# Scoring the diagonal and far ends of a sliding window together with whole key tiles, as tiles of 32 by 64

## The chip, the cores and the metric

The kernel runs on one core of a Trainium2 chip. The metric is the time of one execution on the device in microseconds; the median of a few runs counts. The core has a matrix engine (PE, with its weight loads listed apart as PEld), a vector engine (DVE), a scalar engine that makes the exponentials (ACT), a general engine (POOL) and a queue that issues most transfers (SP). They run at the same time and wait for each other by semaphores; each takes its own instructions in order. Matrix products write to PSUM, the other tensors lie in SBUF.

## The reference

Two attention layers over 2048 tokens, 640 wide, 32 heads of 20, whose outputs stand side by side.

```python
# A: four segments of 512 tokens; causal softmax inside a segment, and a memory of the segments before
logits = einsum('bhqd,bhkd->bhqk', qs, ks) * scale + mask
a_dot = einsum('bhqk,bhkd->bhqd', softmax(logits), vs)
a_mem = (phi(qs) @ M) / (phi(qs) @ z + 1e-6)
o = g * a_mem + (1.0 - g) * a_dot          # g = sigmoid(beta), one for each head
M = M + phi(ks)^T @ vs;  z = z + sum(phi(ks))
# B: sliding window of 256 keys
mask = (i - j >= 0) & (i - j < 256)
p = softmax(where(mask, q @ k^T * scale, -1e9));  o = p @ v
# both: out = o @ wo
```

## The kernel before

The work is cut into eight chunks of 512 tokens, in the order A0, B0, A1, B1, A2, B2, A3, B3. For each chunk the queries, keys and values are projected (`qk_job`, `v_job`), scores are made, turned into exponentials and masked (`score_batch`, `mask`), multiplied by the values (`av`, `av_tile`), transposed and divided by the sum (`turn`, `norm`), and projected to the output (`final`, `final_job`). Projections of the next chunk and output projections of earlier ones are put between the scores of the present chunk.

Heads have 20 rows, so four heads lie in the four row groups of 32 of the matrix engine; there are eight such groups of four heads. One **visit** of `score_batch` takes two PSUM tiles `sc` of 128 by 2 by 512 (three exist), runs score matmuls for the four heads of one or more groups into up to 512 columns of each head, and then one exponential on ACT for each of the two tiles. The results are two tiles `pt` (ten exist), in which masks set the forbidden scores to zero.

In B the keys are stored shifted by 64, so that a whole key tile `("f", u)` covers the keys from 64 before query block u to its middle. A query block of 128 needs two whole tiles of 128 keys and two **ends**: the upper half of its own diagonal, 64 keys by its last 64 queries (`"l"`, into PSUM rows 0 to 63), and the far 64 keys by its first 64 queries (`"u"`, into rows 64 to 127). Whole tiles run as matmuls on tiles of 32 rows by 128 columns of the engine, ends as tiles of 32 by 64.

For chunks B0 to B2, `batches` makes five visits for each pair of groups. In the order of issue they are

```python
(g0,   f0 256 queries, f3 128, f-1 128)   # f-1 not in chunk 0
(g0,   f1 256,         f2 256)
(both, ends of all four query blocks)      # 16 entries of 64 queries, 64 matmuls
(g0+1, f0, f3, f-1)
(g0+1, f1, f2)
```

After the third visit the first group's value product may run, after the fifth the second's. In whole-tile visits two kinds of mask are selects on POOL (line 862): `near`, at the lower edge of the diagonal, and `far`, at the far edge of the window, each over two blocks of 64 queries and both heads of a tile, 256 elements. The ends are masked by one multiply on DVE (line 840) with a table `ends`. A's chunks and B's last chunk have visits of ends alone too; there the change leaves the work as it is.

The order of all matrix work is written out in `PLAN`, a list that the main loop of `body` follows: `S` and `s` are the next visit, `A` the next value product, `M` the next memory product, `q30*5` five matmuls of that projection, and so on. An `A` behind an `S` makes the projections after it run as four column tiles of 128 by 32, the shape that the value product has, in place of one of 128 by 128; that saves a change of shape and issues four times the instructions. Each engine gets its instructions in the order in which this loop emits them; what isn't in the list (masks, copies, divisions, transfers) is placed by a running estimate, `Flow`, that holds assumed times of every engine.

Lines named below: 807 the score matmuls, 823 the exponentials, 862 the selects, 840 the multiplies of ends, 876 and 898 the value products, 929 and 924 the projections (as one matmul and as four column tiles), 943 the transposes, 981 the products with the reciprocal sum.

Of the kernel before, what the change touches and what calls it, by code (L numbers as in the profile page):

```python
# [13 lines left out]
P = 128  # L14
H = 32
DH = 20
# [251 lines left out]
class _K:  # L268
# [526 lines left out]
    def score_batch(self, n, ent, kof, q, masks):  # L795
# [3 lines left out]
        cols = 0  # L799
        for g, ref, q0, nq, c0 in ent:  # L800
            k, kc = kof(ref)
            h0, h1 = {"a": (0, P), "f": (0, P), "l": (0, SH), "u": (SH, P), "s": (0, SH),
                      "t": (SH, P)}[ref[0]]
            k0 = kc + (h0 if ref[0] != "t" else 0)
            for j in range(4):
                rows = slice(HD * j, HD * j + DH)
                nc.tensor.matmul(ps[j // 2][h0:h1, j % 2, c0:c0 + nq],  # L807
                                 lhsT=k[rows, g, k0:k0 + h1 - h0],
                                 rhs=q[rows, g, q0:q0 + nq],
                                 start=True, stop=True, tile_position=(HD * j, h0),  # L810
                                 skip_group_check=ref[0] in "lust")
# [22 lines left out]
    def mask(self, m, pt, te, ready, x):  # L834
        nc, f = self.nc, self.f
        kind, c0, n = m
        if kind == "ends":
            def go():
                blk = pt[:, :, 0:n].rearrange("p h (b c) -> p h b c", c=SH)
# [15 lines left out]
        else:  # L855
            blk = pt[:].rearrange("p h (b c) -> p h b c", c=2 * P)[:, :, 0:n, c0:c0 + SH]
# [320 lines left out]
    def batches(self, chunks):  # L1177
# [5 lines left out]
        near = lambda n: ("near", 0, n)  # L1183
        far = lambda n: ("far", P + SH, n)
        for n, (kind, c) in enumerate(chunks):
            if kind == "A":
                for g0, ng, at in SQUARES0 if c == 0 else SQUARES:
                    for g in range(g0, g0 + ng):
                        for ent in BANKS_A:
                            out.append([n, [(g, ("a", kt), P * kt + SH, L - P * kt - SH, c0)  # L1190
                                            for kt, c0 in ent], [("part", c0, SH) for _, c0 in ent], []])
                        if g == g0 + at:
# [3 lines left out]
                                        [("ends", 1, P * ng)], []])  # L1196
# [7 lines left out]
            if n == len(chunks) - 1:  # L1204
                for qt in range(LT):
                    for g0 in (0, 2, 4, 6):
# [5 lines left out]
                        if g0 == 2:  # L1212
                            out.append([n, [e for g in range(G) for e in ends(g, qt, SH * g)],
                                        [("ends", 0, L)], [(qt, 0)]])
# [494 lines left out]
```

## Time and profile before

| what | us |
|---|---|
| median of three runs | 329.65 |
| the runs | 329.33, 329.65, 332.19 |
| the profiled execution | 332.08 |
| its span, first to last instruction | 330.4 |
| PE busy | 319.3 |
| ACT busy | 300.2 |
| POOL busy | 266.4 |
| DVE busy | 256.9 |

The profile is one execution. Busy time of PE is the union of its matmuls, each with its latency, so it doesn't say that PE streams all that time; the other engines run one operation at a time. A row of the timeline has the start and the length of one or more like instructions, then the engine, the line, the operation and the shapes, with the idle time before it in brackets and what ended it. PE's granted clock was 0.995 of full speed over the span. The chunks show in the operands of the scores: B0 is scored from 47 to 90 us, B1 from 126 to 170, B2 from 204 to 246, B3 from 280 on.

### The profile page before, as it was taken

To read this page: it belongs to the slowest core of one execution; us is meant where nothing else is said; L and a number is where in the kernel's file an instruction comes from. 1 tells how busy PE (TensorE), PEld (TensorE's weight loads), DVE (VectorE), ACT (ScalarE), POOL (GpSimd) and SP (SyncE) were. 2 spreads that over 40 slices of the span, in tenths; PEclk is the share of its full clock that TensorE was granted. 3 is DMA by queue.
4 is the path that set the end of the run, shared out by engine and by line. 5 is a ranking of instruction groups with operands and counts; after the bars stand their busy time and mean duration, and the time that the engine had idled before them with its cause. 6 is when DMAs were issued, how large, how long until landed. Compare 5 with 4: busy or idle time off the path is not lost.

```text
span 330.4 us, 17022 instructions
## 1 busy us (share of the span) xinstructions
PE 319.3 (97%) x7218; PEld 177.5 (54%) x7218; DVE 256.9 (78%) x537; ACT 300.2 (91%) x334; POOL 266.4 (81%) x676
## 2 busy tenths in 40 slices
PE   8999999999999999999999999999999999979995
PEld 2455546455544455656654546456754545646673
DVE  6777667789887878898868887889667798846673
ACT  2889899899999997999999999899999999949972
POOL 8376679988759989987877999998976899958870
PEclk9999999999999999999999999999999999979999
DMA  6985854743568867264699146057674064577412
GB/s 188 406 257 136 190 148 107 170 138 65 116 164 180 183 146 209 45 138 114 170 170 221 35 87 183 8 113 161 146 175 100 11 178 125 117 190 167 101 64 81
DMA packets 73449, 47.12 MB, mean 143 GB/s; under 512 B 47229, under 2 KB 70045, under 8 KB 73373
## 3 DMA queue, kind: packets, MB, share of 16 engines
q1 hardware_dynamic: 72653, 45.38, 55.8%
q8 instruction: 56, 0.92, 1.2%
q10 hardware_dynamic: 720, 0.66, 0.7%
q14 instruction: 20, 0.16, 0.2%
HBM read 17.62 MB, written 16.79 MB: 104 GB/s over the span
## 4 chain that ended last, share of the span: by engine, by line
PE 61%; POOL 16%; ACT 8%; issue 7%; DVE 4%; DMA 3%; POOLq 0%; ACTq 0%; DVEq 0%
PE m L929 30%; PE sc L807 13%; POOL pt L862 10%; PE m L924 9%; PE m L876 8%; ACT pt L823 7%; POOL o L981 3%; DMA wv_A<-in_A_wv_dram 2%; POOL u L981 2%; DVE tt L943 1%; ACT e L577 1%; DMA wk_A<-in_A_wk_dram 1%; PE m L686 1%; DVE pt L840 1%; POOL pkS L668 1%
## 5 line engine op out<-in xcount | busy, mean ns | idle before, releaser
L823 ACT ACTIVATE pt<-sc 128x1024 bf16<-128x1024 f32 (+2 forms) x306 | 283.4, 1017 | 14.6 <-PE sc L807 12.4
L862 POOL TENSOR_SCALAR_AFFINE_SELECT pt<-pt 128x128 bf16<-128x128 bf16 (+1 forms) x512 | 178.8, 378 | 49.2 <-ACT pt L823 42.5
L943 DVE STREAM_TRANSPOSE tt<-m 128x512 f32<-128x512 f32 x88 | 61.5, 711 | 24.2 <-PE m L876 13.4
L981 POOL TENSOR_TENSOR o<-tt,rr 128x320 bf16<-128x320 f32 x64 | 48.4, 756 | 4.6 <-DVE rr L971 3.9
L807 PE MATMUL sc<-qB,kB 20*64 20x64 bf16 (+2 forms) x1728 | 40.8, 218 | 2.7 <-issue 2.0
L840 DVE TENSOR_TENSOR pt<-pt,ends 128x1024 bf16<-128x1024 bf16 (+2 forms) x50 | 37.4, 758 | 0.0
L1093 DVE CAST ot<-m 128x320 bf16<-128x320 f32 x58 | 27.8, 484 | 11.6 <-PE m L929 9.9
L807 PEld LDWEIGHTS <-kB 20*64 20x64 bf16 (+1 forms) x1728 | 22.6, 99 | 25.6 <-issue 23.2
L929 PEld LDWEIGHTS <-xT 128*128 128x128 bf16 x295 | 26.4, 97 | 18.2 <-issue 6.3
L807 PE MATMUL sc<-qA,kA 20*64 20x64 bf16 (+4 forms) x1024 | 34.2, 237 | 0.2 <-issue 0.2
L929 PEld LDWEIGHTS <-oT 128*128 128x128 bf16 x239 | 21.5, 99 | 11.3 <-issue 1.6
L807 PEld LDWEIGHTS <-kA 20*128 20x128 bf16 (+1 forms) x1024 | 14.0, 97 | 21.9 <-issue 19.9
L929 PE MATMUL m<-wBv,xT 128*128 128x320 bf16 x145 | 24.0, 299 | 1.1 <-DVE tt L943 0.6
L876 PE MATMUL m<-pt,vA 128*32 128x192 bf16 (+3 forms) x512 | 23.6, 274 | 0.0
L929 PE MATMUL m<-wo_A,oT 128*128 128x320 bf16 x131 | 23.2, 312 | 0.0
L929 PE MATMUL m<-wv_A,xT 128*128 128x320 bf16 x130 | 22.0, 300 | 0.3 <-DMA wv_A<-in_A_wv_dram 0.3
L929 PE MATMUL m<-xT,wq_A 128*128 128x512 bf16 x85 | 21.5, 380 | 0.7 <-DMA wq_A<-in_A_wq_dram 0.6
L929 PE MATMUL m<-xT,wBk 128*128 128x512 bf16 x84 | 21.5, 381 | 0.0
L929 PE MATMUL m<-xT,wBq 128*128 128x512 bf16 x77 | 20.3, 380 | 0.0
L738 DVE CAST vB<-m 128x320 bf16<-128x320 f32 x32 | 15.6, 487 | 4.7 <-PE m L929 2.4
L557 DVE CAST kB<-m 128x512 bf16<-128x512 f32 x20 | 13.7, 686 | 6.4 <-PE m L929 4.6
L981 POOL TENSOR_TENSOR u<-tt,rr 128x320 bf16<-128x320 f32 x24 | 18.0, 753 | 0.2
(127 smaller groups left out, 458.6 us busy)
## 6 DMA issues: line engine op xcount, KB each, us to landing
out_dram<-ot SPq DMA_DIRECT2D x29, 160.0 KB
scr_o<-o SPq DMA_DIRECT2D x28, 160.0 KB
xT<-in_B_x_dram SPq DMA_DIRECT2D x8, 288.0 KB
xT<-in_A_x_dram SPq DMA_DIRECT2D x8, 256.0 KB
scr_pk<-e SPq DMA_DIRECT2D x15, 128.0 KB
vS<-vA SPq DMA_DIRECT2D x16, 87.0 KB
vL<-vB SPq DMA_DIRECT2D x8, 174.0 KB
vU<-vB SPq DMA_DIRECT2D x14, 87.0 KB
```

The source lines that it names most:

```text
L557: nc.vector.tensor_copy(out=dst[:, m, at:at + L], in_=ps[:, :])
L738: nc.vector.tensor_copy(out=dst, in_=src)
L807: nc.tensor.matmul(ps[j // 2][h0:h1, j % 2, c0:c0 + nq], lhsT=k[rows, g, k0:k0 + h1 - h0], rhs=q[rows, g, q0:q0 + nq], start=True, stop=Tr ...
L823: nc.scalar.activation(out=pt[:, :, lo:hi], in_=ps[i][:, :, lo:hi], func=ACT.Exp, scale=self.scale)
L840: nc.vector.tensor_tensor(out=blk, in0=blk, in1=self.ends[:, c0, :].unsqueeze(1).unsqueeze(1) .to_broadcast([P, 2, n // SH, SH]), op=ALU.mult)
L862: nc.gpsimd.affine_select(out=blk, in_=blk, pattern=pat, compare_op=ALU.is_ge, fill=self.zero, base=base, channel_multiplier=mul)
L876: nc.tensor.matmul(O[HD * j:HD * j + HD, q0:q0 + nq], lhsT=v[:, at:at + HD], rhs=pts[j // 2][:, j % 2, c0:c0 + nq], start=(n_ == 0), stop= ...
L924: self.nc.tensor.matmul(ps[s, 0:n], lhsT=lhsT[:, s], rhs=rhs, start=start, stop=stop, tile_position=(0, HD * j), skip_group_check=True)
L929: self.nc.tensor.matmul(ps[:, 0:n], lhsT=lhsT, rhs=rhs, start=start, stop=stop, skip_group_check=True)
L943: self.nc.vector.transpose(out=tt[:], in_=O[:, :])
L981: nc.gpsimd.tensor_tensor(out=to[:] if add_to else to, in0=a, in1=b, op=ALU.mult)
L1093: nc.vector.tensor_copy(out=ot[:, 320 * hf:320 * hf + 320], in_=ps[:, 0:320])
```

## The change

For chunks B0 to B2 the five visits of a pair become

```python
(g0,   f1 256, f3 128,  ends of query blocks 0 and 1)
(g0,   f2 256, f-1 128, ends of query blocks 2 and 3)   # f-1 not in chunk 0
(both, f0 256 of each group)
(g0+1, f1, f3, ends of 0 and 1)
(g0+1, f2, f-1, ends of 2 and 3)
```

In a visit that has ends, whole key tiles are scored as two halves of 64 keys, so that the whole visit is in tiles of 32 by 64: 16 matmuls for two whole key tiles and 16 for four ends. The third visit has whole tiles alone, on tiles of 32 by 128. The mask of ends is multiplied into 128 of a tile's columns from a given start, and `near` and `far` get the step between their blocks as a parameter, with one or two blocks each. The assumed time of visits on tiles of 32 by 64 is another one, and `PLAN` is another list, with the same number of each kind of entry but for one `S` that became `s`.

```diff
 PLAN = (
-    "q00*5 k00*5 k01*5 s q01*5 v00*4 S v00*14 s v00*2 q02*3 S q02*2 q03*5 k02*3 S k02*2 k03*5 "
...
+    "k00*5 q00*5 q01*5 S k01*5 v00*5 S v00*10 s v00*5 k02*5 s q02*5 k03*3 S k03*2 q03*5 k04*5 A "
...
+        by_half = ent[-1][1][0] in "lust"
         for g, ref, q0, nq, c0 in ent:
             k, kc = kof(ref)
-            h0, h1 = {"a": (0, P), "f": (0, P), "l": (0, SH), "u": (SH, P), "s": (0, SH),
-                      "t": (SH, P)}[ref[0]]
-            k0 = kc + (h0 if ref[0] != "t" else 0)
-            for j in range(4):
-                rows = slice(HD * j, HD * j + DH)
-                nc.tensor.matmul(ps[j // 2][h0:h1, j % 2, c0:c0 + nq],
-                                 lhsT=k[rows, g, k0:k0 + h1 - h0],
...
+            halves = {"l": (0,), "s": (0,), "u": (SH,), "t": (SH,)}.get(ref[0], (0, SH) if by_half else (0,))
+            w = SH if by_half else P
+            for h0 in halves:
+                k0 = kc + (h0 if ref[0] != "t" else 0)
+                for j in range(4):
+                    rows = slice(HD * j, HD * j + DH)
+                    nc.tensor.matmul(ps[j // 2][h0:h0 + w, j % 2, c0:c0 + nq],
+                                     lhsT=k[rows, g, k0:k0 + w],
...
-        if ent[0][1][0] in "lust":
-            t = f.on_pe("row64", 40.0 * len(ent), cols / 2, 0.0, 4 * len(ent))
+        if by_half:
+            ends = sum(e[1][0] in "lust" for e in ent)
+            mms = 4 * (2 * len(ent) - ends)
+            ns = max(20.8 * ends + (cols - SH * ends) / 2.4 + 5.0, 0.0 if mms <= 32 else 8.35 * mms - 8.0)
+            t = f.on_pe("row64", ns, cols / 2, 0.0, mms)
...
-                blk = pt[:, :, 0:n].rearrange("p h (b c) -> p h b c", c=SH)
+                blk = pt[:, :, at:at + n].rearrange("p h (b c) -> p h b c", c=SH)
...
-            blk = pt[:].rearrange("p h (b c) -> p h b c", c=2 * P)[:, :, 0:n, c0:c0 + SH]
+            x0 = c0 // at
+            blk = pt[:].rearrange("p h (b c) -> p h b c", c=at)[:, :, x0:x0 + n, c0 % at:c0 % at + SH]
...
             for g0 in range(0, G, 2):
                 for g in (g0, g0 + 1):
-                    ent = [(g, ("f", 0), 0, 2 * P, 0), (g, ("f", 3), 3 * P, P, 2 * P)]
-                    if c > 0:
-                        ent.append((g, ("f", -1), 0, P, 3 * P))
-                    out.append([n, ent, [near(2), far(2 if c else 1)], []])
-                    out.append([n, [(g, ("f", 1), P, 2 * P, 0), (g, ("f", 2), 2 * P, 2 * P, 2 * P)],
-                                [near(2), far(2)], []])
+                    for x in range(2):
+                        ent = [(g, ("f", 1 + x), P + P * x, 2 * P, 0)]
+                        if x == 0:
+                            ent.append((g, ("f", 3), 3 * P, P, 2 * P))
+                        elif c > 0:
+                            ent.append((g, ("f", -1), 0, P, 3 * P))
+                        c0 = 2 * P if x else 3 * P
+                        out.append([n, ent + [e for qt in (2 * x, 2 * x + 1)
+                                              for e in ends(g, qt, c0 + SH * (qt % 2))],
+                                    [near(1 if x else 2), far(2 if x and c else 1),
+                                     ("ends", 0, P, c0)], []])
                     if g == g0:
-                        out.append([n, [e for x in range(2) for qt in range(LT)
-                                        for e in ends(g0 + x, qt, 256 * x + SH * qt)],
-                                    [("ends", 0, L)], [g0]])
+                        out.append([n, [(g + y, ("f", 0), 0, 2 * P, 2 * P * y) for y in range(2)],
+                                    [near(2), far(2)], [g0]])
                 out[-1][3].append(g0 + 1)
```

More of the change, by code (lines that the diff above doesn't have):

```diff
@@ L799, in score_batch @@
         cols = 0
+        by_half = ent[-1][1][0] in "lust"
         for g, ref, q0, nq, c0 in ent:
             k, kc = kof(ref)
-            h0, h1 = {"a": (0, P), "f": (0, P), "l": (0, SH), "u": (SH, P), "s": (0, SH),
-                      "t": (SH, P)}[ref[0]]
-            k0 = kc + (h0 if ref[0] != "t" else 0)
-            for j in range(4):
-                rows = slice(HD * j, HD * j + DH)
-                nc.tensor.matmul(ps[j // 2][h0:h1, j % 2, c0:c0 + nq],
-                                 lhsT=k[rows, g, k0:k0 + h1 - h0],
-                                 rhs=q[rows, g, q0:q0 + nq],
-                                 start=True, stop=True, tile_position=(HD * j, h0),
-                                 skip_group_check=ref[0] in "lust")
-            cols += nq
-        if ent[0][1][0] in "lust":
-            t = f.on_pe("row64", 40.0 * len(ent), cols / 2, 0.0, 4 * len(ent))
+            halves = {"l": (0,), "s": (0,), "u": (SH,), "t": (SH,)}.get(ref[0], (0, SH) if by_half else (0,))
[6 more added lines that the diff above has]
+                                     lhsT=k[rows, g, k0:k0 + w],
+                                     rhs=q[rows, g, q0:q0 + nq],
+                                     start=True, stop=True, tile_position=(HD * j, h0),
+                                     skip_group_check=by_half)
+            cols += nq
+        if by_half:
[3 more added lines that the diff above has]
+            t = f.on_pe("row64", ns, cols / 2, 0.0, mms)
         else:
@@ L1182, in batches @@
         out = []
-        near = lambda n: ("near", 0, n)
-        far = lambda n: ("far", P + SH, n)
+        near = lambda n, step=2 * P: ("near", 0, n, step)
+        far = lambda n, step=2 * P: ("far", P + SH, n, step)
         for n, (kind, c) in enumerate(chunks):
@@ L1190, in batches @@
                             out.append([n, [(g, ("a", kt), P * kt + SH, L - P * kt - SH, c0)
-                                            for kt, c0 in ent], [("part", c0, SH) for _, c0 in ent], []])
+                                            for kt, c0 in ent], [("part", c0, SH, 0) for _, c0 in ent], []])
                         if g == g0 + at:
@@ L1195, in batches @@
                                             for x in range(ng) for kt in range(LT)],
-                                        [("ends", 1, P * ng)], []])
+                                        [("ends", 1, P * ng, 0)], []])
                         if g >= g0 + at:
@@ L1213, in batches @@
                             out.append([n, [e for g in range(G) for e in ends(g, qt, SH * g)],
-                                        [("ends", 0, L)], [(qt, 0)]])
+                                        [("ends", 0, L, 0)], [(qt, 0)]])
                     out[-1][3].append((qt, 4))
```

2 lines of the change are left out of this document (1 added, 1 removed), and 42 rows, old and new, of the table PLAN.

## The prediction

> **What bounds the kernel now.** First the page: how busy each engine is, and what the chain that ended last is made of.
>
> ```profile
> span 330.4 us, 17022 instructions
> ...
> PE 319.3 (97%) x7218; PEld 177.5 (54%) x7218; DVE 256.9 (78%) x537; ACT 300.2 (91%) x334; POOL 266.4 (81%) x676
> ...
> PE 61%; POOL 16%; ACT 8%; issue 7%; DVE 4%; DMA 3%; POOLq 0%; ACTq 0%; DVEq 0%
> ...
> L823 ACT ACTIVATE pt<-sc 128x1024 bf16<-128x1024 f32 (+2 forms) x306 | 283.4, 1017 | 14.6 <-PE sc L807 12.4
> ```
>
> PE is named first, but its 97% contains the overlapped latency of short matmuls. ACT's 91% is real: 306 exponentials of 1017 ns, in order. They idle 14.6 us in all, 12.4 us of it until PE had written scores. A saving on PE can therefore be paid out only where ACT waits for PE. So I next cut the span into the stretches in which chunks 0, 1 and 2 of B are scored, the only visits that the change touches.
>
> ```profile
> 47.00:90.00 43.00, 42.58 (x996) 23.58 (x979) 36.01 (x74) 41.77 (x50) 37.38 (x87) 1.00 0.53 130
> ...
> 126.00:170.00 44.00, 43.50 (x1117) 26.02 (x1108) 38.15 (x81) 41.37 (x46) 38.41 (x82) 1.00 0.54 142
> ...
> 204.00:246.00 42.00, 41.85 (x1113) 24.79 (x1109) 34.34 (x70) 40.02 (x44) 38.07 (x82) 1.00 0.52 114
> ```
>
> Columns: length, then busy time of PE, weight loads, DVE, ACT, POOL, then the granted clock (full, 1.00) and DMA. ACT is free for 1.2, 2.6 and 2.0 us; POOL for 5.6, 5.6 and 3.9 us; DVE for 7.0, 5.9 and 7.7 us. Who ended ACT's waits in the three stretches, one after the other (total, times, longest):
>
> ```profile
> ACT pt L823 <- POOL one L437: 0.7, 1, 0.7
> ACT pt L823 <- PE sc L807: 0.3, 1, 0.3
> ...
> ACT pt L823 <- PE sc L807: 2.7, 5, 1.0
> ...
> ACT pt L823 <- PE sc L807: 1.8, 4, 0.9
> ```
>
> PE is late by 0.3, 2.7 and 1.8 us. Those 4.8 us are the most that faster scoring in these stretches can return by itself.
>
> **The change, part by part.** *Scoring on PE.* A pair of head groups has five visits before and after. Before, four hold whole key tiles (8 to 12 matmuls) and one holds the 64 small ones. After, four hold 32 matmuls each (24 in two per pair of chunk 0), all on tiles of 32 by 64, and one holds 8 whole-tile matmuls. The listings of both programs give 7218 matmuls before and 7612 after: 352 more for scoring, 42 more because some projections run as four column tiles. They change tile shape 337 and 335 times, so nothing is gained or lost there that counts. What a visit occupies is read from its start to the start of what follows:
>
> ```profile
> 59.87 0.84 PE L807 MATMUL sc<-qB,kB 20*64 20x64 bf16 x64
> 60.64 0.39 PE L929 MATMUL m<-xT,wk_A 128*128 128x512 bf16 x1
> 60.86 2.11 PE L929 MATMUL m<-xT,wq_A 128*128 128x512 bf16 x9
> 62.90 0.34 PE L807 MATMUL sc<-qB,kB 20*128 20x256 bf16 x8
> ...
> 64.80 0.40 PE L807 MATMUL sc<-qB,kB 20*128 20x256 bf16 x8
> 65.12 1.05 PE L924 MATMUL m<-xT,wk_A 128*32 128x512 bf16 x16
> ...
> 71.00 0.71 PE L807 MATMUL sc<-qB,kB 20*64 20x64 bf16 x64
> 71.64 0.39 PE L929 MATMUL m<-xT,wq_A 128*128 128x512 bf16 x1
> ```
> ```profile
> 13.32 0.33 PE L807 MATMUL sc<-qA,kA 20*64 20x64 bf16 x32
> 13.58 0.45 PE L929 MATMUL m<-wv_A,xT 128*128 128x320 bf16 x2
> ```
> ```profile
> 51.06 0.75 PE sc L807 x64
> ...
> 125.92 0.71 PE sc L807 x64
> ...
> 160.50 0.78 PE sc L807 x64
> ```
>
> A whole-tile visit takes 0.32 us (64.80 to 65.12). The 64 small matmuls take 0.77 and 0.64 us, and 0.75, 0.71 and 0.78 in the chain: mean 0.73. For the new visit the nearest row is the one of 32 small matmuls in A: 0.26 us. It streams 4 times 64 columns through each of the eight tiles; the new visit streams 256+128+64+64 = 512. A column costs 0.44 ns (nine matmuls of 512 in 2.04 us, 60.86 to 62.90), so 256 more cost 0.11: **0.37 us**. Bounds: at least 0.32, since a whole-tile visit streams the same 512 columns per row group; at most 0.48, if every matmul costs the 12 ns of the slowest 64-visit (0.77/64, 32 of them 0.38) behind a shape change, which I take as 0.10. I take 0.37, from the row that is like it in count and tile.
>
> Per pair: before 4x0.32+0.73 = 2.01; after 4x0.37+0.32 = 1.80; saved 0.21 us (bounds +0.41 and -0.23). Four pairs to a stretch: 0.84 us. Twelve pairs: 2.5 us (+4.9 to -2.8). Against ACT's waits for PE this pays min(0.3, 0.84) + 0.84 + 0.84 = **2.0 us**.
>
> The Trainium skill's page "TensorEngine Tiling (Array Packing)", Performance Considerations, warns against this very step: every matmul carries about 60 cycles, so one shouldn't take a tiling factor from a size that is already small. As an estimate from that page, 25 ns for each of 32 in line would be 0.8 us a visit, and the kernel some 18 us slower. The trace speaks against it as long as tiles overlap: 10 to 12 ns per matmul in the rows of 64.
>
> *Exponentials.* Same number and same columns in the sum of a pair (in chunk 0 the visit with 384 columns is another one). Nothing.
>
> *Selects on POOL and multiplies on DVE.* Each visit fills two tiles of exponentials. The mask of the ends was two multiplies of 1024 elements a pair, one for each tile of that visit; now eight tiles have one of 256 each. Selects: 16 of 256 elements a pair become 12 of 256 and 8 of 128. By the listings 48 more selects and 72 more multiplies.
>
> ```profile
> L862 POOL TENSOR_SCALAR_AFFINE_SELECT pt<-pt 128x256 bf16<-128x256 bf16 x240 | 100.9, 450 | 22.7 <-ACT pt L823 19.6
> L862 POOL TENSOR_SCALAR_AFFINE_SELECT pt<-pt 128x128 bf16<-128x128 bf16 x272 | 78.9, 313 | 26.5 <-ACT pt L823 22.9 <-PE m L929 2.1
> ```
> ```profile
> L840 DVE TENSOR_TENSOR pt<-pt,ends 128x1024 bf16<-128x1024 bf16 x44 | 34.5, 793 | 0.0
> ...
> L840 DVE TENSOR_TENSOR pt<-pt,ends 128x768 bf16<-128x768 bf16 x4 | 2.2, 549 | 0.0
> ...
> L840 DVE TENSOR_TENSOR pt<-pt,ends 128x512 bf16<-128x512 bf16 x2 | 0.8, 417 | 0.0
> ```
>
> One select of 256 split in two costs 2x313-450 = 176 ns more: 16 per stretch, 2.8 us, 8.4 in all. A multiply of 256 isn't in the trace; 417 minus the 132 by which 512 and 768 differ gives 0.29 us as an estimate (bounds 0.20, a quarter of the 793 of the longest, and 0.42, the shortest one seen). Per pair 8x0.29 instead of 2x0.79: 0.7 us, 3 us a stretch. Cover: POOL's 5.6, 5.6, 3.9 us and DVE's 5.9 us or more. So I cost both at nothing, but in the third stretch POOL then is at 38.07+2.8 = 40.9 of 42, over ACT's 40.0: the cover is thin. In return the two multiplies of 0.8 us in one visit, which hold up PSUM copies, become short ones.
>
> *A wait moves.* The value product of a pair's first group waited last for the ends' multiply on DVE; now its third visit is the whole-tile one, so it waits for four selects on POOL. PE runs in order: behind a held product stand the next projections and the next visit, and behind that ACT.
>
> *Fetching instructions.* PE's own instructions come in blocks.
>
> ```profile
> q8 instruction: 56, 0.92, 1.2%
> ```
> ```profile
> 291.38 0.59 PE L807 MATMUL sc<-qB,kB 20*64 20x64 bf16 x50
> 293.93 0.31 PE L807 MATMUL sc<-qB,kB 20*64 20x64 bf16 x14 [1.96 <-issue]
> 294.18 0.71 PE L929 MATMUL m<-wo_A,oT 128*128 128x320 bf16 x2
> ```
> ```profile
> 294.29 1.94 ACT L823 ACTIVATE pt<-sc 128x1024 bf16<-128x1024 f32 x2 [3.94 <-PE sc L807]
> ```
>
> 0.92 MB in 56 packets is 16 KB each, for 14436 weight loads and matmuls: about 256 a block. 788 more make three more blocks. In the last chunk of B a visit of 64 stands 2 us in its middle, and ACT 3.9 us behind it. That stretch keeps its visits of 64.
>
> *Order.* The new list has the same numbers of every piece, and the value products stand behind the same visits as before. Projections are shifted by a few matmuls between visits; no stretch gains or loses a projection chain. The DMA issues on SP are equal in number (318 copies, 12 transposes); near the start the key store and the square copy change places. Two fewer shape changes: 0.2 us. I cost the rest at nothing, within 1 us either way.
>
> **The sum.** The profiled execution took 332.08 us: 330.4 of span and 1.7 around it. The timed runs were 329.33, 329.65 and 332.19; two levels, 2.5 us apart, and I read the profile as one on the upper level, whose likeliest content is the stop at 291. So 332.08 - 2.0 - 0.2 = 329.9 with that stop, and 329.9 - 2.4 = **327.4** on the level of the median, 329.65.
>
> **The rivals.**
> *1. The order pays out more.* All 4.8 us of ACT's waits for PE go, and 1 us, the most I gave the order: 329.65-5.8 = 323.9. For it: even visits feed ACT evenly, and the bursts of 0.8 us on DVE go. Against: a long wait of the third stretch stands where A gives way to B, not behind a visit of 64:
>
> ```profile
> 210.16 1.94 ACT L823 ACTIVATE pt<-sc 128x1024 bf16<-128x1024 f32 x2 [0.87 <-PE sc L807]
> ```
>
> *2. ACT and the queues bound it; nothing is paid.* What PE saves becomes waiting for score buffers: 329.65, and 332 when the stop recurs in the median run.
> *3. Slower: POOL takes over.* The place is the value product of each pair's first group, and the third stretch above all; it decides from the point at which POOL's sum (40.9) passes ACT's (40.0). If half of the 8.4 us of selects reaches PE in order, that is 4.2 us, and PE's saving has no one to use it: 329.65+4.2 = 333.9. The row of selects of 256 shows a mean of 450 ns where the shortest is 411:
>
> ```profile
> L862 POOL TENSOR_SCALAR_AFFINE_SELECT pt<-pt x512: 288/411/934, 10.0 to 320.4; 128x128 bf16<-128x128 bf16 x91, 128x256 bf16<-128x256 bf16 x80
> ```
>
> (minimum, median and maximum over both sizes: single ones are held to 0.9 us). The Trainium skill's "GPSIMD Engine Reference", Specifications, has POOL share its SBUF interface with DVE operations of two SBUF inputs, which the ends' multiplies are; if that is what holds single selects, 72 more of them hold more.
> *4. Slower: each small matmul has its price, however its tiles overlap.* The 12 ns of the slowest visit of 64 make 0.48 us a visit; PE loses 0.23x12 = 2.8 us: 332.5. Against it: the 32 of A, 0.26 us, behind a shape change too. That is the mechanism of the page on tiling at the price that the rows show.
>
> **How the numbers follow.** Forecast 327.4 with its own range 325 to 329 (the order's 1 us, PE's bounds cut by ACT's waits): chance 0.38. Rival 1: 0.25. Rival 2: 0.12. Rival 3: 0.17. Rival 4: 0.08. A measurement of this kernel tells about 1%, 3.3 us, from no change: below 326.35 lies rival 1 and a third of the forecast's range, 0.38; above 332.95 lie rival 3, part of 4 and of 2, 0.24; between them 0.38. The range 323.5 to 333.5 leaves out the far half of rivals 1 and 3, and holds the rest.
>
> **What would show it.** Right: new visits of 32 at 0.35 to 0.38 us from start to start; ACT's waits for PE in the three B stretches down from 4.8 to under 3 us; POOL 2.8 us busier in each. Wrong: visits near 0.48; ACT's waits unchanged or ended by PE behind a product that POOL released; a stop of PE inside a visit at a new place; a multiply of 256 above 0.42 us.

## The result and the profile after

The changed kernel takes **338.85 us** (median of four runs, 338.18 to 339.74) against 329.49 of the kernel before, measured beside it (327.78 to 332.19). The ratio is 1.0268, 95% interval 1.0214 to 1.0321: slower by 9.4 us, where 327.4 was predicted and 333.5 was the upper end of the range. The profiled execution took 339.74. Runs that were some per cent slower at a lower granted clock than the others of their kernel are left out of the medians in this document; that concerns two of e2's four runs and one run of the kernel before.

The page of the kernel after: span, busy time, the chain that ended last by engine, the exponentials, and the multiplies of ends with their count, busy time and mean.

```profile
span 338.0 us, 17910 instructions
...
PE 319.0 (94%) x7612; PEld 181.4 (54%) x7612; DVE 268.9 (80%) x609; ACT 299.8 (89%) x334; POOL 271.9 (80%) x724
...
PE 74%; DVE 13%; ACT 5%; issue 4%; DMA 3%; POOL 0%; POOLq 0%; SPq 0%; ACTq 0%; DVEq 0%
...
L828 ACT ACTIVATE pt<-sc 128x1024 bf16<-128x1024 f32 (+2 forms) x306 | 283.0, 1026 | 23.3 <-PE sc L809 20.0
...
L845 DVE TENSOR_TENSOR pt<-pt,ends 128x256 bf16<-128x256 bf16 (+3 forms) x122 | 52.7, 443 | 0.3 <-ACT pt L828 0.2
```

Busy time hardly tells it: PE 319.0 as before (319.3), ACT 299.8 (300.2). What has changed is that ACT waits for scores 20.0 us in place of 12.4, and that the chain goes through DVE for 13% in place of 4% and through POOL no more (16% before). Multiplies of ends were 37.5 us before (34.5+2.2+0.8) and are 52.7 now.

The three stretches of the kernel after in which B0, B1 and B2 are scored (columns as in the prediction):

```profile
46.50:90.00 43.50, 41.91 (x1087) 24.57 (x1082) 38.45 (x95) 41.76 (x50) 39.26 (x103) 1.00 0.62 140
121.60:170.00 48.40, 44.93 (x1291) 28.25 (x1288) 44.57 (x109) 43.98 (x49) 42.05 (x103) 1.00 0.55 143
205.60:251.00 45.40, 43.22 (x1260) 27.24 (x1256) 39.03 (x97) 41.41 (x45) 40.46 (x102) 1.00 0.50 125
```

And what the exponentials waited for in them, one after the other (total, times, longest):

```profile
ACT pt L828 <- PE sc L809: 1.2, 3, 0.5
...
ACT pt L828 <- PE sc L809: 4.4, 6, 1.7
...
ACT pt L828 <- PE sc L809: 3.7, 7, 1.4
```

That is 9.3 us in place of 4.8. (These stretches begin at the first score of a chunk. The stretches of the kernel before began later, at 126 and 204 us, where its first scores of B1 and B2 stand at 121.2 and 200.3; begun there, its waits are the same 2.7 and 1.8.) So the waits which the change was forecast to shorten have doubled, although PE's own work is as short as forecast. That is read from the start of a new visit and of what follows it (kernel after, timeline of PE; the two rows are neighbours):

```profile
55.92 0.44 PE L809 MATMUL sc<-qB,kB 20*64 20x256 bf16 x32
56.29 0.72 PE L935 MATMUL m<-wBv,xT 128*128 128x320 bf16 x4
```

A visit of 32 occupies 0.37 us. So PE isn't slow, it waits. For whom, over the whole span, after (total, times, longest):

```profile
PE m L935 <- DMA oT<-scr_o: 3.1, 1, 3.1
PE m L882 <- issue: 2.0, 1, 2.0
PE m L935 <- DVE tt L949: 1.5, 6, 0.4
PE m L935 <- DVE vA L733: 1.2, 1, 1.2
PE m L935 <- DVE ot L1099: 1.2, 2, 0.6
PE m L882 <- DVE qA L557: 1.0, 1, 1.0
PE m L930 <- DVE vA L733: 0.9, 2, 0.6
```

and all its waits for DVE before:

```profile
PE m L929 <- DVE tt L943: 0.6, 3, 0.2
...
PE m L924 <- DVE qB L557: 0.2, 1, 0.2
PE m L924 <- DVE qA L557: 0.2, 1, 0.2
```

Two things stand out. One wait of 3.1 us for a transfer stands near the end, where the change was said to leave the work as it is. And PE waits for DVE 5.8 us in the rows shown (7.3 with five more of 0.2 to 0.5), against 1.0. The stop of 2.0 ("issue") has its like before, the stop inside a visit at 291 that the prediction quotes.

**The wait near the end**, in the timeline of the kernel after: SP's transpose, PE's five matmuls that need it, and the exponentials behind.

```profile
307.27 2.77 SPq L1044 DMA_TRANSPOSE oT<-scr_o  x1
...
313.65 1.18 PE L935 MATMUL m<-wo_A,oT 128*128 128x320 bf16 x5 [3.11 <-DMA oT<-scr_o]
...
315.50 1.94 ACT L828 ACTIVATE pt<-sc 128x1024 bf16<-128x1024 f32 x2 [3.22 <-PE sc L809]
```

The new list puts the first five matmuls of A3's output projection (`o60*5`) ahead of a visit of B3, one visit earlier than the old one. (Visits are counted over the whole kernel, 153 in all, by their exponentials.) Their input comes through a transposing transfer that is issued at 307.27 and on which PE stands until 313.65, and ACT behind it. Before, the last transpose into `oT` was issued 10 us earlier. Counted in visits, it was issued during the 142nd before and during the 145th after, so the transfer is later as well as its reader earlier:

```profile
297.64 2.59 SPq L1038 DMA_TRANSPOSE oT<-scr_o  x1
```

The stop costs more than its 3.1 us. Behind it PE runs at a lower granted clock, the column before the last two (kernel after; it is 1.00 from 305 to 314 and from 318 to 322):

```profile
314.00:316.00 2.00, 2.00 (x56) 1.23 (x58) 0.49 (x1) 0.50 (x1) 0.00 (x0) 0.51 0.93 205
316.00:318.00 2.00, 2.00 (x61) 1.31 (x53) 0.77 (x2) 1.44 (x2) 1.28 (x4) 0.64 0.40 113
```

That takes some 1.7 us of PE's time, 2x(0.49+0.36), as an estimate. Counted by the starts of exponentials, the changed kernel is 3.5 us behind the kernel before at the 147th visit (310.33 and 306.79) and 8.1 at the 152nd (324.34 and 316.20): in this trace the tail loses 4.6 us. The two stops of 2.0 us have the same behind them: the clock is 0.52 and 0.62 from 174 to 178 us in the kernel after, and 0.50 from 294 to 297 in the kernel before.

**A wait in B1.** DVE's instructions one after the other, and PE's row that waited for the last of them:

```profile
137.14 0.49 DVE L733 TENSOR_TENSOR vA<-m,omg 128x320 bf16<-128x320 f32 x1
137.55 0.44 DVE L592 TENSOR_SCALAR pq<-qA 128x512 bf16<-128x512 bf16 x1
138.02 0.43 DVE L598 TENSOR_TENSOR pq<-pq,e 128x512 bf16<-128x512 bf16 x1
138.36 0.82 DVE L592 TENSOR_SCALAR pq<-qA 128x512 bf16<-128x512 bf16 x1
139.21 0.42 DVE L598 TENSOR_TENSOR pq<-pq,e 128x512 bf16<-128x512 bf16 x1
139.56 0.49 DVE L733 TENSOR_TENSOR vA<-m,omg 128x320 bf16<-128x320 f32 x1
...
140.10 0.84 PE L935 MATMUL m<-wv_A,xT 128*128 128x320 bf16 x5 [1.21 <-DVE vA L733]
```

PE needs the PSUM tile `m` that the copy `vA` of 139.56 frees. Between it and the copy before stand four operations for A's memory, which no one is waiting for. DVE has no gap here, so the copy is late, and with it PE, the next scores and ACT: by the starts of exponentials the changed kernel is level with the kernel before at the 65th visit (139.23 and 139.31) and 2.0 us behind at the 68th (148.54 and 146.57). No multiply stands among these operations. In f1 below, where the multiplies are cut short, the wait at this place is still there; in f2, where the selects are, it is 0.6:

```profile
138.44 0.84 PE L936 MATMUL m<-wv_A,xT 128*128 128x320 bf16 x5 [1.25 <-DVE vA L733]
```

So the length of the multiplies isn't enough to explain this one wait.

### The profile page after: what moved, and what is told of

It reads as the page before. It is cut to its first block, busy times and chain, and to the rows that moved or that the text cites. A ratio compares the mean times of both kernels' runs of the same rounds, so it can differ in the third digit from the quotient of the medians.

```text
span 338.0 us, 17910 instructions
## 1 busy us (share of the span) xinstructions
PE 319.0 (94%) x7612; PEld 181.4 (54%) x7612; DVE 268.9 (80%) x609; ACT 299.8 (89%) x334; POOL 271.9 (80%) x724
## 4 chain that ended last, share of the span: by engine, by line
PE 74%; DVE 13%; ACT 5%; issue 4%; DMA 3%; POOL 0%; POOLq 0%; SPq 0%; ACTq 0%; DVEq 0%
PE m L935 38%; PE sc L809 14%; PE m L930 10%; PE m L882 8%; ACT pt L828 5%; DVE tt L949 3%; DVE pt L845 2%; DMA oT<-scr_o 2%; PE m L904 2%; DMA xT<-in_A_x_dram 1%; PE m L686 1%; DVE qA L557 1%; DVE pq L598 1%; DVE vA L733 1%; DVE pq L592 1%
## 5 line engine op out<-in xcount | busy, mean ns | idle before, releaser
L828 ACT ACTIVATE pt<-sc 128x1024 bf16<-128x1024 f32 (+2 forms) x306 | 283.0, 1026 | 23.3 <-PE sc L809 20.0
L868 POOL TENSOR_SCALAR_AFFINE_SELECT pt<-pt 128x128 bf16<-128x128 bf16 (+1 forms) x560 | 186.7, 361 | 45.4 <-ACT pt L828 41.1
L845 DVE TENSOR_TENSOR pt<-pt,ends 128x256 bf16<-128x256 bf16 (+3 forms) x122 | 52.7, 443 | 0.3 <-ACT pt L828 0.2
L809 PE MATMUL sc<-qB,kB 20*64 20x64 bf16 (+4 forms) x2080 | 37.0, 222 | 0.6 <-ACT pt L828 0.6
L809 PEld LDWEIGHTS <-kB 20*64 20x64 bf16 (+1 forms) x2080 | 24.0, 102 | 22.6 <-issue 21.1
L935 PEld LDWEIGHTS <-xT 128*128 128x128 bf16 x282 | 25.2, 97 | 19.3 <-issue 8.6
L935 PE MATMUL m<-wo_A,oT 128*128 128x320 bf16 x126 | 22.1, 306 | 3.4 <-DMA oT<-scr_o 3.1
L935 PE MATMUL m<-xT,wBk 128*128 128x512 bf16 x86 | 23.7, 397 | 0.0
L935 PE MATMUL m<-xT,wk_A 128*128 128x512 bf16 x70 | 19.2, 397 | 0.5 <-DVE tt L949 0.3
L935 PE MATMUL m<-xT,wq_A 128*128 128x512 bf16 x68 | 17.4, 381 | 0.5 <-DVE tt L949 0.4
```

Source lines behind the costliest of these rows:

```text
L809: nc.tensor.matmul(ps[j // 2][h0:h0 + w, j % 2, c0:c0 + nq], lhsT=k[rows, g, k0:k0 + w], rhs=q[rows, g, q0:q0 + nq], start=True, stop=True ...
L828: nc.scalar.activation(out=pt[:, :, lo:hi], in_=ps[i][:, :, lo:hi], func=ACT.Exp, scale=self.scale)
L845: nc.vector.tensor_tensor(out=blk, in0=blk, in1=self.ends[:, c0, :].unsqueeze(1).unsqueeze(1) .to_broadcast([P, 2, n // SH, SH]), op=ALU.mult)
L868: nc.gpsimd.affine_select(out=blk, in_=blk, pattern=pat, compare_op=ALU.is_ge, fill=self.zero, base=base, channel_multiplier=mul)
L935: self.nc.tensor.matmul(ps[:, 0:n], lhsT=lhsT, rhs=rhs, start=start, stop=stop, skip_group_check=True)
```

## The experiments

Medians below stand against 328.4 to 329.1 us of the kernel before, measured beside them. A profiled execution can lie about 2 us off the median of its kernel, so times are compared by medians, and traces are used for the place. In the expectations, O stands for the order as the cause and D for VectorE.

### Which half of the change loses the time?

`e1`: the new visits with the old list. `e2`: the old visits with the new list.

```diff
 e1:  kernel after, PLAN = that of before
 e2:  kernel before, PLAN = that of after
```

> The visits of the changed kernel with the order list of the kernel before. Theory O (the new order does the harm: an output projection placed ahead of its transpose, a stop for instructions at another place): 327 to 330 us, at or below before. Theory D (the 72 more small multiplies load DVE, whose PSUM copies hold PE): 333 us or more, with the waits of PE for DVE in B1 and B2 that the changed kernel has.

> The visits of the kernel before with the new order list. Theory O: 335 us or more, with the wait for the transposed output near 313 us. Theory D: within 2 us of before, 328 to 332 us.

Measured: e1 339.48 us (ratio 1.0314, 1.0253 to 1.0374), e2 347.2 (1.0534, 1.0452 to 1.0615). Neither half is harmless, and together they lose less than the sum. As single causes both theories fall: the new visits are slow without the new list, and the new list is slower still without the visits that it was made for. Neither time is the price of one half alone: in e1's trace PE stops for 3.8 us at three scores with nothing shown that it waits for (2.2 before), and e2's has a wait of 3.6 us for a transpose into `oT`. So the next runs take the changed kernel and alter one place.

### The tail of the order

`e3` takes the order of before from visit 132 on, the last chunk. `g1` makes a single exchange in the new list:

```diff
-... s o50*2 o60*5 s A o60*5 s o70*5 o50*5 s A ...
+... s o50*2 o50*5 s A o60*5 s o70*5 o60*5 s A ...
```

> The changed kernel with the old order from visit 132 on (the last chunk of B, visits numbered from 1). Leaves the first 280 us as they are. If the 3.3 us in which PE waits for the transposed output at 313 us come from the order there: 334.5 to 336 us. If that wait is only slack taken from what follows: 338 us or more.

> The changed kernel with one exchange in its order: the first five matmuls of the output projection of A's last block (o60*5), which stand ahead of visit 149 and wait 3.11 us for the transposed copy of its outputs, change places with five matmuls of the chunk before (o50*5) that stand one visit later. Everything else is as in the changed kernel. Theory 'the order of the tail' (4.5 us of the loss come from that one wait): the wait is gone and the time is 334 to 335.5 us, near the 333.62 of the run with the whole old tail. Theory 'the tail was only where a lateness from the B stretches showed': another wait takes its place and the time stays at 337.5 to 339.

Measured: e3 333.62 us (1.0128, 1.0068 to 1.0188), g1 334.26 (1.0143, 1.0098 to 1.0188). Ten matmuls that change places return 4.6 us of the 9.4, as much as the trace gave the tail. The wait at 313 is gone, and g1's granted clock is 1.00 over the whole execution; a wait of 1.67 us for the transpose before it, at 300.31, is in this trace. The exponentials of g1, to be compared with 23.3 and 20.0:

```profile
L828 ACT ACTIVATE pt<-sc 128x1024 bf16<-128x1024 f32 (+2 forms) x306 | 283.0, 1025 | 18.9 <-PE sc L809 15.7 <-POOL pt L868 1.9
```

The tail's part is settled. Of the runs that follow, those that alter the changed kernel start from e3, but for e4; so 4.6 us are left to be explained. e3's profiled execution, 331.73, is its fastest, so its trace shows less than that.

### Multiplies and selects: without, or cut short

`e4` leaves the 96 multiplies of B0 to B2 out of the changed kernel. `f1` cuts them to 8 elements in e3, `f2` cuts the 192 selects of the visits with ends to 2 of 64 columns, `h3` does both. These kernels, and h1 and h2 below, leave part of the masks undone. In f1, f2 and h3 the order of matmuls stays.

```diff
 e4: -  near(...), far(...), ("ends", 0, P, c0)
     +  near(...), far(...)
 f1: +  w = 2 if at else SH          # columns of each block that are multiplied
 f2: +  near(...) + (2,), far(...) + (2,)   # columns that are selected
```

> The changed kernel without the 96 multiplies that mask the ends in B0 to B2; the ends stay unmasked there, so this part of the computation is left out. DVE loses 37 us of work, more than the kernel before spent there (20 us). Theory D: the loss in B1 and B2 (3.5 us by the starts of visits) goes, 333 to 335 us. Theory O: 337 us or more.

> The changed kernel with the old order for the last chunk, and each of the 96 small multiplies of B0 to B2 cut from 256 to 8 elements, in the same place of the same order; the ends stay unmasked but for two of 64 columns. Takes some 20 us of work from DVE and nothing else. Theory D (DVE's added work holds PE in B1 and B2): 330.5 us or less, 3 us or more under the same kernel with whole multiplies (333.6). Theory O (the order alone): within 1 us of 333.6.

> The same kernel with the 192 selects of the visits with ends in B0 to B2 cut to two columns of 64 each, in the same place; the masks of whole key tiles stay almost undone there. Takes some 40 us of work from POOL. If POOL's selects were what holds the value products: 331 us or less. Theories D and O: 332.5 to 334.

> The old tail's order with both the 96 multiplies cut to 8 elements and the 192 selects to 2 of 64 columns, order unchanged. Leaves most of the ends' multiplication and masks undone. If the matmuls' saving of the prediction (2.0 us paid out) stands ready once the ends cost nothing: 326.5 to 327.7 us. If it doesn't, since the exps or the order set the pace of the B stretches: 328.7 to 329.5 us.

Measured: e4 336.75 us (1.0199, 1.0132 to 1.0265), 2.1 less than the changed kernel, with a wait of 2.9 us for the same transpose still in it. f1 330.75 (1.0028, 0.9988 to 1.0068), f2 329.27 (0.9994, 0.9957 to 1.0031), h3 328.92 (0.9992, 0.9965 to 1.0019). Short multiplies return 2.9 us, short selects 4.3, both together 4.7: not a sum. That would be so if they acted through one thing, and also if the time of the kernel before, 329, were a floor. The rows of the multiplies on DVE show one thing that both act on. First those of the changed kernel, then f1's, then f2's:

```profile
L845 DVE TENSOR_TENSOR pt<-pt,ends 128x256 bf16<-128x256 bf16 x96 | 35.8, 385 | 0.3 <-ACT pt L828 0.2
```
```profile
L846 DVE TENSOR_TENSOR pt<-pt,ends 128x8 bf16<-128x8 bf16 x96 | 22.1, 241 | 0.7 <-ACT pt L828 0.6
```
```profile
L846 DVE TENSOR_TENSOR pt<-pt,ends 128x256 bf16<-128x256 bf16 x96 | 29.1, 314 | 0.7 <-ACT pt L828 0.7
```

A multiply of 8 elements still takes 241 ns in the mean, and one of 256 falls from 385 to 314 when only POOL's selects get shorter. So a multiply is held while a select runs. Sorted one by one in the trace of the changed kernel, the 7 multiplies of 256 that overlap no operation of POOL take 267 ns in the mean and at most 282; the 85 that overlap a select take 388 in the mean and up to 806. The Trainium skill's "GPSIMD Engine Reference", Specifications, says that POOL shares its SBUF interface with DVE operations that read two SBUF inputs; these rows agree with it.

h3 also tells what became of the matmuls' saving. The same visit of B1, the 61st, starts 2.0 us earlier than before (first row before, second row h3):

```profile
129.79 1.94 ACT L823 ACTIVATE pt<-sc 128x1024 bf16<-128x1024 f32 x2 [0.95 <-PE sc L807]
```
```profile
127.79 1.94 ACT L828 ACTIVATE pt<-sc 128x1024 bf16<-128x1024 f32 x2 [0.68 <-PE sc L809]
```

Of these 2.0 us 0.6 is older than B0, whose first visit, the 20th, starts at 47.62 in place of 48.21, and at the 65th visit 1.5 us are left. The medians are alike (328.92 against 329.09). h3's waits of PE for DVE over the span:

```profile
PE m L937 <- DVE tt L951: 1.4, 6, 0.4
PE m L937 <- DVE ot L1101: 1.1, 3, 0.6
...
PE m L937 <- DVE pt L847: 0.9, 3, 0.5
...
PE m L937 <- DVE vA L733: 0.6, 1, 0.6
```

With five more of 0.2 they are 5.0 us, against 1.0 before. Even with almost nothing to multiply and select, PE comes to tiles that DVE hasn't copied yet. In this execution 1.5 us of these waits stand between 205 and 240 us, where before has none, and there the lead ends: it is 1.2 us at the 100th visit (208.97 and 210.16) and nothing at the 113th (237.88 and 237.78). ACT also waits 0.8 us for selects in that stretch, so the copies needn't be the only cause.

### VectorE's time, or the lateness of the ends?

f1 takes load off DVE and lets the selects and the value products begin sooner. `h1` puts the load back without the lateness: a multiply of 192 elements on a spare tile behind each short one. `h2` does the like for f2 on POOL.

```diff
 h1 (f1, behind each multiply of 8):
+    nc.vector.tensor_tensor(out=spare, in0=spare, in1=ends, op=mult)     # 3 x 64 elements
 h2 (f2, behind each short select):
+    nc.gpsimd.affine_select(out=spare, in_=spare, ...)                   # 2 or 3 x 64 elements
```

> The run with multiplies cut to 8 elements (330.75 us), with a multiply of 192 elements on a spare tile behind each of the 96 in VectorE's order; nobody reads that tile, so the selects and the value products don't wait for it. VectorE is as busy as with whole multiplies; the ends are as early as with short ones. Leaves most of the ends' multiplication undone, as that run did. Theory 'VectorE's time': 333 to 335 us, as with whole multiplies (333.62). Theory 'lateness of the ends': 330.5 to 331.5 us.

> The run with selects cut to 2 of 64 columns (329.27 us), with a select of 128 or 192 elements on the spare tile behind each of the 192 in POOL's order. POOL is busier than with whole selects, by its fixed part of some 0.17 us a select, 33 us in all, and the value products wait for the short ones only (a short one still stands behind the spare ones before it). Leaves most of the masks of these visits undone, as that run did. Theory 'time of POOL, and of VectorE held behind it': 333 us or more. Theory 'lateness of the ends': 329.5 to 331 us. Well above 336 says only that POOL is now overfull.

Measured: h1 334.02 us (1.0139, 1.0103 to 1.0175); h2 342.4 (1.0401, 1.0373 to 1.0429). h1 takes back the whole 2.9 us of f1, though nothing waits for what was added: DVE's time is enough of a cause. Two cautions: DVE is 273.8 us busy in h1, 5.3 more than in e3, so the load was put back with some to spare; and in h1 one product waits 1.1 us for a select. h2 lies above 336, where its expectation says that POOL is overfull, so it tells only that POOL has no room either. How much of f2's 4.3 us came through the shorter holding of DVE, and how much through POOL's own queue, isn't separated.

### The same work in fewer instructions

Both tiles `pt` of a visit lie in one tile, so that one multiply of 512 elements does for two of 256 (`g2`, from e3; the multiplies of visits of ends alone merge too, which the expectation doesn't say: 13 instead of 26). In `g3` the selects are merged as well, in `g4` those of the kernel before. `h4` holds the tiles in pairs and merges nothing.

```diff
-            pt = piece("pt", NPT, (P, 2, 512))           # for each i of 2
+        both = piece("pt", NPT // 2, (P, 4, 512))
+            pt = both[:, 2 * i:2 * i + 2, :]
+            if merged and i == 1: mask(m, both, ...)     # four heads in one instruction
```

> The run with the old tail, its order unchanged, with the two exp tiles of a visit held as one tile, so that the ends of a visit are multiplied by one VectorE instruction of 512 elements instead of two of 256 (48 instead of 96 in the B stretches). The same work is done. Theory 'the multiplies' (each costs a fixed part of VectorE's time and stands behind POOL's selects): a multiply of 512 takes 0.45 to 0.6 us against two of 0.38, VectorE is busy some 10 us less, and the time is 330.7 to 332.5 us. Theory 'not the multiplies': 333 to 334 us as without it; more than that if the one multiply, which starts only behind the second exp, delays the value products.

> As the run with merged multiplies, and the selects of both exp tiles of a visit also made by one POOL instruction (half as many, twice as long). The same work is done. Theory 'POOL's fixed part per select': POOL is busy some 15 us less in all and VectorE is held less, 329 to 331.5 us. Rival: the select now starts only when the second exp has ended, and the value products stand behind it: 333 us or more.

> The kernel before, its order unchanged, with the selects of both exp tiles of a visit made by one POOL instruction. The same work is done. If POOL's fixed part per select costs the kernel before anything, 327.5 to 328.5 us; if it has cover there, as its 48 selects cut in two (1.0047) suggest, within 1 us of 329; if the later start of the merged select holds the value products, 331 us or more.

> The old tail's order with the two exp tiles of a visit as one tile in memory, and nothing merged: a control for the runs with merged multiplies (337.15) and merged both (338.32). Theory 'the merged multiply is late' (it starts only behind the second exp): 333 to 334.5 us, as without pairs. Theory 'pairs come free later, and the exps wait for them': 336 us or more.

Measured: g2 337.15 us (1.0245, 1.0214 to 1.0276), g3 338.32 (1.0274, 1.0227 to 1.0321), g4 333.24 (1.012, 1.009 to 1.015), h4 333.4 (1.011, 1.0066 to 1.0153). Pairs alone cost nothing (333.62 without). Merging does what it should on DVE (260.2 us busy in place of h4's 269.2) and still loses 3.8 us. The multiplies of the B stretches and the selects in g2 and then in g3:

```profile
L854 DVE TENSOR_TENSOR pt<-pt,ends 128x512 bf16<-128x512 bf16 x48 | 23.0, 480 | 1.0 <-ACT pt L833 0.8
...
L877 POOL TENSOR_SCALAR_AFFINE_SELECT pt<-pt 128x128 bf16<-128x128 bf16 x368 | 109.4, 318 | 30.6 <-ACT pt L833 28.7
L877 POOL TENSOR_SCALAR_AFFINE_SELECT pt<-pt 128x256 bf16<-128x256 bf16 x192 | 83.7, 455 | 12.1 <-ACT pt L833 10.7
```
```profile
L854 DVE TENSOR_TENSOR pt<-pt,ends 128x512 bf16<-128x512 bf16 x48 | 27.0, 563 | 0.8 <-ACT pt L833 0.7
...
L877 POOL TENSOR_SCALAR_AFFINE_SELECT pt<-pt 128x256 bf16<-128x256 bf16 x184 | 81.9, 462 | 53.1 <-ACT pt L833 51.9 <-POOL o L996 0.4
L877 POOL TENSOR_SCALAR_AFFINE_SELECT pt<-pt 128x512 bf16<-128x512 bf16 x96 | 66.9, 712 | 25.2 <-ACT pt L833 20.5 <-PE m L944 2.4 <-PE sc L812 1.8
```

My theory of the multiplies said 330.7 to 332.5 for g2; it falls as a theory of DVE's sum. The loss shows at the selects, though g2 doesn't merge them: ACT waits 4.4 us for them in place of h4's 1.6, and PE has waits for them of which e3 and h4 have none. That it comes from the merged multiply starting only behind the second exponential fits, but isn't shown. PE's waits for selects in g2:

```profile
PE m L891 <- POOL pt L877: 2.2, 3, 1.0
```

g3 shows the holding from the other side: the same multiply of 512 takes 563 ns beside selects of 462 and 712 ns, and 480 beside those of 318 and 455. g4 loses 4 us against the kernel before though POOL is less busy (225.7 us in place of 266.4); its trace shows PE waiting for copies, and that the later start of the select does it isn't shown.

### Small masks in the kernel before

`f3` cuts the 24 multiplies of 1024 elements in B0 to B2 in four each, `f4` cuts 48 selects of 256 in two.

> The kernel before with each of the 24 multiplies of 1024 elements in B0 to B2 cut into four of 256, one behind the other: the changed kernel's multiplies in number and size, everything else as before. Theory D: 332 us or more. Theory O: 328.5 to 331.

> The kernel before with 48 selects of 256 elements in B0 to B2 cut into two: the changed kernel's number of selects. If 8.4 us more on POOL cost time by themselves: 331.5 us or more. Theories D and O: 328 to 331.

Measured: f3 342.33 us (1.0354, 1.0273 to 1.0435); f4 330.72 (1.0047, 1.0005 to 1.009). The same elements in 72 more multiplies cost the old kernel 13 us; a part of that is a stop of PE of 2.0 us inside a visit, like the one at 291 before, which f3's trace has too. f3's PE waits for DVE's copies up to 2.0 us at a time; the two longest rows are

```profile
PE m L927 <- DVE qA L557: 3.4, 4, 1.5
...
PE m L932 <- DVE kA L557: 2.0, 1, 2.0
```

The 48 more selects, the number that the change adds, cost 1.8 us by the medians (0.2 to 3.0 by the interval); POOL's busy time rose from 266.4 to 275.7.

### Can the place in VectorE's queue be mended?

With e3's order of matmuls, `i1` changes one number of the planner, `i2` the rule by which the first multiply of a visit is placed.

```diff
 i1: -  ready[x] = f.on_dve(72.0 + 1.036 * n, te, True)
     +  ready[x] = f.on_dve(385.0 if at else 72.0 + 1.036 * n, te, True)
 i2: -  if x % 2:
     +  if x % 2 or at:
            f.when_idle(te, go)
```

> The old tail's order, whole work, with one number of the planner changed: a small multiply is counted at 385 ns, as measured, in place of 205. The matmuls' order stays; VectorE's instructions, some of POOL's and of the DMA queue's move. Theory 'the copies stand at a wrong place in VectorE's queue, since the planner thinks the multiplies short': 329 to 331.5 us. Theory 'the multiplies' time itself': 332.5 to 334.5 us, as without (333.62).

> The old tail's order, whole work; the first multiply of a visit is placed like the second, when VectorE's queue has a gap, and not at a fixed time before its exp ends. The matmuls' order stays. Theory 'the copies that PE waits for stand behind multiplies': they go ahead more often, 330 to 332.5 us. Theory 'the ends must be early': the selects and the value products come later, 335 us or more.

Measured: i1 339.72 us (1.0306, 1.022 to 1.0392), i2 334.74 (1.0145, 1.0069 to 1.022). Neither mends it, and the truer price makes it 6 us worse. i1's exponentials wait for selects, in e3 1.4 us:

```profile
ACT pt L828 <- PE sc L809: 15.1, 23, 1.9
ACT pt L828 <- POOL pt L868: 5.5, 8, 1.9
```

So the queue's order matters by several microseconds, as this run shows in the wrong direction. A list of matmuls searched anew with a price of 385 ns wasn't tried, and no run that does the whole work beat the kernel before.

## Why the prediction was wrong

*The bound.* "A saving on PE can therefore be paid out only where ACT waits for PE" holds, and so does the place: ACT's waits for scores are 7.6 us longer (20.0 against 12.4), and the two profiled executions are 7.7 us apart (339.74 and 332.08). But the step took those waits as something that only PE's scoring sets. They are as much what DVE, POOL and a transfer let PE do.

*Scoring on PE: right in size, not in pay.* A visit of 32 was put at 0.37 us and takes 0.37. The 0.8 that I had estimated from the Trainium skill's "TensorEngine Tiling (Array Packing)", Performance Considerations, with the overhead of all 32 in line, isn't borne out: the tiles overlap. The term "2.0 us paid" fails: with ends that cost almost nothing (h3) the kernel gains 0.2 us, interval -0.6 to 1.2. A lead was there in B1, 1.5 to 2.0 us with 0.6 of it older than B0, and it was gone in B2, where PE waits 1.5 us for copies and ACT 0.8 for selects.

*Selects and multiplies "at nothing": the first step that failed*, by 4.7 us (e3 against h3). It failed twice. The multiply was mis-sized: 0.29 us predicted, 0.385 measured. For a multiply by itself 0.29 was close (0.267 where POOL does nothing); what it left out is the holding, which the prediction names only for selects. And the cover was counted as DVE's idle sum over a stretch: 5.9 us in B1 against 3 us of more work. The idle sum did fall as reckoned: begun at B1's first score, the stretch has 7.2 us before (48.80-41.63, from 121.2 to 170) and 3.8 after (48.40-44.57). But idle time elsewhere in 48 us doesn't help a copy that stands in a full queue: PE's waits for DVE rose from 1.0 to 7.3 us. That sum isn't itself the loss: h3 still has 5.0 us of such waits and loses nothing. That the load on DVE and POOL costs the 4.7 us is shown by f1, f2, h1 and h3; which single waits pay how much of it stays open.

*The order "within 1 us either way": the second step that failed*, by 4.6 us at one place (g1). I compared the number of pieces in the stretches, not the distance between a transfer's issue and its first reader. The list shows five matmuls of `o60` one visit earlier, and the trace of before has the transpose that they read as a row of its own; the step looked at neither. Nor did it reckon that a stop of 3.1 us would cost 4.6, with the clock at 0.51 and 0.64 behind it.

*A wait moves.* PE's waits for selects at the value products didn't appear: none in the changed kernel, and POOL left the chain (16% to 0%).

*Fetching instructions.* One stop of 2.0 us before, one after, at other places, each with the slow clock behind it: no part of the 7.7 us between the two profiled executions. In the medians it may have a part. A profiled execution with one such slow stretch has a granted clock of 0.995 (before), one with two 0.990 (after); the changed kernel's four executions have 0.990 three times and 0.995 once, where one stretch is the tail's. That the stops are instruction fetches isn't shown.

*The rivals.* Rival 3, slower with POOL as its root, had the sign, and with 333.9, by luck, the size of what is left without the tail (333.62). Its place was wrong: PE waits not at value products behind POOL, but mostly at projections behind DVE's copies. POOL still has its share, since shorter selects alone return 4.3 us. Rival 2's time is near h3's (329.65 and 328.92), but its mechanism isn't there: PE waits 0.3 us for score buffers in h3. Rival 4 falls with the visits at 0.37. The tail of the order had no rival at all, so the range was 5 us short.

## What to carry to other kernels

When work is cut finer on the engine that is bound, count what the finer cut adds on the engines behind it, at the price of an operation in traffic and not by itself: a multiply of 8 elements took 241 ns here beside busy selects. Idle time of an engine is cover only where the queue has a gap at the moment when someone waits, so read it at the places where its results free the next tile. And when an order is searched anew, look at every first use of a transferred tile: ten matmuls were worth 4.6 us, some 1.5 of them through the slower clock behind the stop.

## What the runs showed of the hardware

A DVE operation with two SBUF inputs is stretched while POOL runs selects: 385 ns for 256 elements, 314 with shorter selects; 480 and 563 ns for 512 beside shorter and longer ones. For a short operation it is a large part of the price, which wasn't expected. In f1, whose row of all multiplies follows (minimum, median, maximum in ns), the shortest of 8 elements takes 98 ns, the five that overlap no operation of POOL take 135 in the mean, and the mean of all 96 is 241.

```profile
L846 DVE TENSOR_TENSOR pt<-pt,ends x122: 98/251/1161, 15.4 to 313.6; 128x8 bf16<-128x8 bf16 x96, 128x1024 bf16<-128x1024 bf16 x20, 128x768 bf16<-128x768 bf16 x4, 128x512 bf16<-128x512 bf16 x2
```

And 32 small matmuls of 64 to 256 columns on eight tiles take 0.37 us together, some 12 ns each.

Behind a stop of PE of 2.0 to 3.1 us the granted clock was 0.50 to 0.64 for 3 to 4 us, at all three such stops of the two profiled executions; behind g1's wait of 1.67 us it stayed at 1.00.
